# Ordering weight conversions and pooling around the row maxima of an attention and two feed-forward layers

## Chip, core and metric

One Trainium2 chip, one of its cores. The metric is device time in microseconds (us) of one execution; shorter is better.

## The reference

Pooled attention over 4 batches of 8 heads (1152 rows, head size 64), then two feed-forward layers on the 2304 pooled rows, all in float32:

```python
q_pool = q.reshape(B, H, S // 2, 2, D).mean(axis=3)
scores = np.matmul(q_pool, k.transpose(0, 1, 3, 2)) / sqrt(D)
scores -= scores.max(axis=-1, keepdims=True)
attn = np.exp(scores)
x = np.matmul(attn / (attn.sum(axis=-1, keepdims=True) + 1e-09), v)
x = x.transpose(0, 2, 1, 3).reshape(2304, 512)
h = x @ w_in;  x = (h - tanh(h)) @ w_out               # 512 -> 2048 -> 512
r = np.maximum(x @ w2_in, 0);  out = (s * r * r + b) @ w2_out
```

The kernel keeps float32 accuracy with matmuls of a narrower type by splitting operands into a high and a low part. The feed-forward weights arrive as raw words of two 32-bit halves each and are converted on the chip before they are split.

## The kernel before

The attention stage works on 16 pairs of heads (`n`; four pairs make a batch, `j` is the head in the pair). A head has nine score steps `t`: four matmuls on TensorE (PE) and two exponentials on ScalarE (ACT), into `pf`; every three steps a batch of matmuls multiplies `pf` with the values (`pv`). For the later heads GpSimd (POOL) adds the `pf` into two accumulators (L408), whose columns TensorE then sums; for the first four pairs and the last head TensorE sums them directly.

Around this a clock of ticks runs, four to a score step, so 72 to a pair where nothing stops it. At each tick `tick()` runs the work that has come due in `queue` (put there by `later(k, fn)`, k ticks ahead) and moves on the preparations of later pairs.

A preparation `prep(n)` is begun in pair n - 2, head 1, score step `NKT - LEAD // 4`. It pools the queries (two additions into `qr`, L265, on GpSimd from pair 1 on, and from pair 2 on behind the newest GpSimd addition traced, `added`), pauses four ticks, transposes queries (`ptq`, L271) and keys (`ptk`, L287) on TensorE, takes their low parts on VectorE (DVE; `ql`, `kl`), issues transfers that arrange the operands, and 16 ticks later loads the next pair. After a gap it computes the row maxima: 27 groups of one or two matmuls into a PSUM tile (`ptm`, L316) that VectorE reduces (`mp`, L317). The tag `pp` has three PSUM tiles, shared by maxima, transposes and the sweeps below.

`Weights.step` converts one unit of weights in six VectorE instructions (L195 to L207) from a raw tile (`raw`) that a transfer has filled, the last of them a copy into the weights; GpSimd subtracts for the low part (L210). Two ticks later the next load is traced. `CONVERT` and `CONVERT_AT` place 24 units on score steps of the first 13 pairs, four in each of the first four; 12 more follow in the last pair. A raw tile exists for each load under way: two in attention.

When a head's sum is there, `end` copies it on ScalarE, takes two reciprocals on VectorE (L453), eight ticks later multiplies (L458), splits into `xo` (ScalarE, then GpSimd, L460), and six ticks later stores it to DRAM (L464). From the second pair of the next batch on, a sweep (`sweep1`) loads a batch's results and does part of the first feed-forward layer between the attention's matmuls. After attention come the rest of that layer and then the second, both nearly pure TensorE work.

The framework orders each engine's instructions by priority, which follows the order of the trace, and by when its own model has them ready; an instruction that is ready sooner may be queued ahead of one traced before it. `tc.issue_after(ins)` queues what is traced inside it behind `ins` on the same engine, in order of issue only.

Of the kernel before, what the change touches and what calls it, by code (L numbers as in the profile page):

```python
# [10 lines left out]
F32R = mybir.dt.float32r  # L11
I32 = mybir.dt.int32
AF = mybir.ActivationFunctionType
ALU = mybir.AluOpType
AX = mybir.AxisListType
# [3 lines left out]
P = 128  # L19
# [10 lines left out]
LAST_STEPS = 4  # L30


LEAD = 20
GAP = 30
GAP1 = 12
MAXSTEP = 2
# [2 lines left out]
SUM = 2  # L39
GROUPS = ((0, 1, 2, 3, 4), (5, 6, 7, 8))  # L40
BATCH = 3
STORE, PUT = 8, 6

MOE_NS = 445
EVAC_NS = 250
AHEAD = 400
PFB = 10
SOON = 40
HOLD_NS = 8000
# [2 lines left out]
def f32(ap):  # L52
    return ap.bitcast(F32)
# [3 lines left out]
def attention_moe_moe_kernel(  # L57
# [19 lines left out]
    HB = SQ // 2  # L77
# [19 lines left out]
    act = nc.scalar.activation  # L97
    dve = nc.vector
    pool = nc.gpsimd
# [7 lines left out]
    fp = sctx.enter_context(tc.tile_pool(name="fin", bufs=1, side="right"))  # L107
# [10 lines left out]
    for i in range(4):  # L118
        g = i % 2
# [10 lines left out]

    clock = [0]
    moved = [None]
    added = [None]
    queue = []
    ticking = [True]

    def later(k, fn):
        queue.append((clock[0] + k, fn))
# [10 lines left out]
    def weight(which, f):  # L149
        return slots[w2slot[f] if which else f]  # L150

    class Weights:
# [32 lines left out]
        def step(self):  # L185
            if not self.loaded:
                return
            which, f, i, j, raw = self.loaded.popleft()
            w = weight(which, f)
            cols = slice(j * self.N, (j + 1) * self.N)  # L190
            lo, hi = raw[:, :, 0], raw[:, :, 1]
            t = self.pool.tile([P, self.N], I32, tag="t", name=f"t{which}_{f}_{i}_{j}", bufs=self.bufs)
            x = t.bitcast(F32)

            dve.tensor_scalar(out=t, in0=hi, scalar1=3, scalar2=0x3FFFFFFF,  # L195
                              op0=ALU.logical_shift_left, op1=ALU.bitwise_and)
            dve.scalar_tensor_tensor(out=t, in0=hi, scalar=-0x40000000, in1=t,  # L197
                                     op0=ALU.bitwise_and, op1=ALU.bitwise_or)
            dve.scalar_tensor_tensor(out=t, in0=lo, scalar=29, in1=t,  # L199
                                     op0=ALU.logical_shift_right, op1=ALU.bitwise_or)  # L200

            dve.tensor_scalar(out=hi, in0=hi, scalar1=1, scalar2=-0x80000000,
                              op0=ALU.logical_shift_left, op1=ALU.bitwise_xor)
            dve.scalar_tensor_tensor(out=x, in0=hi, scalar=float(-0x0FE00000), in1=x,
                                     op0=ALU.is_ge, op1=ALU.mult)
            if self.left > self.act_last:
                dve.tensor_copy(w[:, 2 * i, cols], x)  # L207
            else:
                act(w[:, 2 * i, cols], x, AF.Copy)  # L209
            added[0] = pool.tensor_sub(w[:, 2 * i + 1, cols], x, f32(w[:, 2 * i, cols]))  # L210
            later(RELOAD, self.load) if ticking else self.load()
            self.left -= 1
# [43 lines left out]
    def prep(n):  # L256

        T1, Uz, ql = T1s[n % 3], U1s[n % 3], qls[n % 2]
        U1 = [Uz[j][:, QOFF[j]:QOFF[j] + SQ] for j in range(2)]
        ops[n] = (T1, U1)  # L260

        for j in range(2):
            eng = dve if n == 0 else pool
            with tc.issue_after(added[0].ins) if n > 1 else ExitStack():
                eng.tensor_add(qrs[0][:, :, j * D:(j + 1) * D], qrs[j][:, :, 0:D], qrs[j][:, :, D:2 * D])  # L265
        yield 4
        for g in range(2):
            with tc.high_priority(offset=SOON):
                pt = psP.tile([P, KB], F32, tag="pp", name=f"ptq{n}_{g}")
                for i in range(3):  # L270
                    nc.tensor.transpose(  # L271
                        pt[:, i * QP:(i + 1) * QP],
                        qrs[0][:, 3 * g + i],
                        ident[:QP, :QP],
                    )
                act(U1[1][:, g * HB:(g + 1) * HB], pt[:, :HB], AF.Copy)
                dve.tensor_sub(
                    ql[:, g * HB:(g + 1) * HB], pt[:, :HB], f32(U1[1][:, g * HB:(g + 1) * HB])
                )
            yield 2  # L280
        for i in range(2):
            dma(out=f32(U1[0][i * D:(i + 1) * D, :]), in_=f32(U1[1][0:D, :]))
        for g in range(NKB):
            with tc.high_priority(offset=SOON):
                pt = psP.tile([P, KB], F32, tag="pp", name=f"ptk{n}_{g}")
                for i in range(3):
                    nc.tensor.transpose(  # L287
                        pt[:, i * P:(i + 1) * P],
                        kr[:, 3 * g + i].rearrange("p h d -> p (h d)"), ident)
                act(T1[1][:, g * KB:(g + 1) * KB], pt, AF.Copy)  # L290
                dve.tensor_sub(
                    kl[:, g * KB:(g + 1) * KB], pt, f32(T1[1][:, g * KB:(g + 1) * KB])
                )
            yield 2
        dma(out=f32(T1[0][0:D, :]), in_=f32(T1[1][0:D, :]))
        moved[0] = dma(out=f32(T1[0][D:P, :]), in_=f32(kl[0:D, :]))
        with tc.issue_after(moved[0].ins):
            dma(out=f32(U1[1][0:D, :]), in_=f32(U1[1][D:P, :]))
            dma(out=f32(T1[1][0:D, :]), in_=f32(kl[D:P, :]))
        if n + 1 < len(pairs):  # L300
            later(LOAD, lambda: load_pair(n + 1))
        yield GAP1 if n == 1 else GAP
        for j in range(2):
            ns = NQS + 1 - j
            mp = ap.tile([P, ns, NKB], F32, tag=f"mp{j}", name=f"mp{n}_{j}")
            m = ap.tile([P, ns], F32, tag=f"m{j}", name=f"m{n}_{j}")
            for s in range(ns):
                for i in range(NKB):
                    pt = psP.tile([P, KB], F32, tag="pp", name=f"ptm{n}_{j}_{s}_{i}")
                    kk = slice(i * KB, (i + 1) * KB)  # L310
                    if s == NQS:
                        mm(pt, Uz[0][:, s * P:(s + 1) * P], T1[0][:, kk], start=True, stop=False)
                        mm(pt, Uz[1][:, 0:P], T1[1][:, kk], start=False, stop=True)
                    else:
                        q0 = (s + j) * P
                        mm(pt, Uz[j][:, q0:q0 + P], T1[j][:, kk], start=True, stop=True)  # L316
                    dve.reduce_max(mp[:, s, i:i + 1], pt, axis=AX.X)  # L317
                    yield MAXSTEP
            dve.reduce_max(m, mp, axis=AX.X)
            pt = psP.tile([P, KB], F32, tag="pp", name=f"ptc{n}_{j}")  # L320
            nc.tensor.transpose(pt[:ns, :P], m, ident)
            act(cs[j], pt[:ns, :P], AF.Copy, scale=-1.0)
            maxes.add((n, j))
            yield 1
# [85 lines left out]
    def batch():  # L410
# [6 lines left out]
        po = pvt[n, j]  # L417
        with tc.high_priority(offset=AHEAD), tc.issue_after(last[0].ins):
            for i, (_, _, u, pf) in enumerate(reversed(todo)):
# [19 lines left out]
    xvs = {}  # L439
# [6 lines left out]
    def end(n, j, su):  # L446

        b, hp = pairs[n]
        ri = fp.tile([P, HB], F32, tag="ri", name=f"ri{n}_{j}", bufs=2)
        act(ri, su, AF.Copy, bias=1e-9)  # L450
        for g in range(2):
            x = slice(g * HB // 2, (g + 1) * HB // 2)
            dve.reciprocal(ri[:, x], ri[:, x])  # L453

        def store():
            xv = xvs.pop((n, j))
            xo = fp.tile([P, 2, HB], F32R, tag="xo", name=f"xo{n}_{j}", bufs=2)
            dve.tensor_mul(xv, xv, ri)  # L458
            act(xo[:, 0], xv, AF.Copy)
            pool.tensor_sub(xo[:, 1], xv, f32(xo[:, 0]))  # L460

            def put():
                for g in range(2):
                    dma(out=f32(x1d[b][hp][j * D:(j + 1) * D, :, g * HB:(g + 1) * HB]),  # L464
                        in_=f32(xo[g * D:(g + 1) * D]))
                placed.append((n, j))

            later(PUT, put)

        later(STORE, store)  # L470


# [38 lines left out]
    def gate1(pl_, ps, n, nm, bufs):  # L511
# [10 lines left out]

    load_pair(0)
    w1gen = Weights(stage, [[(0, f) for f in range(a, b)] for a, b in ((0, F1), (F1, FW), (FW, FA))],
                    2, 2, 2, LAST_STEPS)
    moe = deque()
    preps = deque()
    pend = deque()
# [43 lines left out]
    for n in range(len(pairs)):  # L572
# [3 lines left out]
        for j in range(2):  # L576
            for t in range(NKT):
                if j == 1 and t == NKT - LEAD // 4 and n + 2 < len(pairs):
                    add_prep(n + 2)
# [165 lines left out]
    for i in range(NBLK):  # L745
# [3 lines left out]
        for f in range(NFC):  # L749
            while w2gen.left > 2 * (NFC - 1 - f):  # L750
# [5 lines left out]
                                     op0=ALU.mult, op1=ALU.mult)  # L756
# [4 lines left out]
                                     op0=ALU.add, op1=ALU.subtract)  # L761
# [35 lines left out]
```

## Time and profile before

| | us |
|---|---|
| median of 3 runs (lowest to highest) | 1428.48 (1426.93 to 1430.91) |
| the profiled execution: its time | 1429.16 |
| its span, first to last instruction | 1427.4 |
| TensorE busy | 1359.7 (95%) |
| VectorE busy | 865.0 (61%) |
| ScalarE busy | 559.6 (39%) |
| GpSimd busy | 385.5 (27%) |

A busy time is that in which the engine runs at least one instruction. Where the engine that is busy nearly all the time waits, the time of the whole is lost; where another waits, nothing need be.

### The profile page before, as it was taken

Reading aid. Unit: us, or ns where it says so; the run is one execution under the profiler, and the core shown is the slowest. Engines: PE = TensorE matmul, PEld = TensorE weight load, DVE = VectorE, ACT = ScalarE, POOL = GpSimd, SP = SyncE. Lnnn points to the kernel's source line nnn. Section 1 sums busy time; section 2 is a strip of 40 time slices with the busy share of each in tenths; the row PEclk is TensorE's granted clock in tenths of the full one; section 3 lists DMA queues with packets and bytes.
Section 4 is the critical chain, followed back from the end, with each engine's and each line's share of the span. In section 5 each row is a group of like instructions: output and inputs, shape, how many; then the busy total and the mean of one; then the engine's idle time right before and its main releaser. Section 6 shows DMA issues by size and latency. Waiting matters only on the chain.

```text
span 1427.4 us, 23107 instructions
## 1 busy us (share of the span) xinstructions
PE 1359.7 (95%) x8670; PEld 1157.2 (81%) x8670; DVE 865.0 (61%) x1640; ACT 559.6 (39%) x1360; POOL 385.5 (27%) x311
## 2 busy tenths in 40 slices
PE   5999898999999999998989998999999999999998
PEld 3666666777777777776989997999899989898997
DVE  7877785667566664759796399844963232323232
ACT  2544445555455544544332233333332222323232
POOL 1212136565556645654220033100210000000000
PEclk9999999999999999999999999999999999999999
DMA  8756655563546555344776134744602020201000
GB/s 196 172 145 160 163 135 139 127 170 92 149 111 164 128 145 143 88 109 139 236 237 220 34 132 158 230 133 147 206 30 67 0 67 0 67 23 44 1 23 23
DMA packets 157647, 169.62 MB, mean 119 GB/s; under 512 B 52064, under 2 KB 130016, under 8 KB 157536
## 3 DMA queue, kind: packets, MB, share of 16 engines
q1 hardware_dynamic: 157536, 168.15, 42.8%
q8 instruction: 68, 1.11, 0.3%
q14 instruction: 43, 0.35, 0.1%
HBM read 101.98 MB, written 30.67 MB: 93 GB/s over the span
## 4 chain that ended last, share of the span: by engine, by line
PE 72%; DVE 16%; DMA 5%; POOL 3%; issue 3%; ACT 1%; SPq 1%; DVEq 0%; POOLq 0%; ACTq 0%
PE h L662 19%; PE o L735 14%; PE pv L421 9%; PE ptm L316 5%; PE y L673 5%; PE s L352 4%; PE s L353 4%; PE y L500 3%; PE h L487 2%; DVE t L199 2%; DMA raw<-in_moe_w_out_dram 2%; DVE t L197 2%; DVE mp L317 2%; DVE t L195 2%; POOL acc L408 2%
## 5 line engine op out<-in xcount | busy, mean ns | idle before, releaser
L662 PE MATMUL h<-xx,w 128*128 128x288 f32 (+1 forms) x2328 | 388.1, 316 | 1.7 <-DVE thb L514 1.7
L662 PEld LDWEIGHTS h<-xx,w 128*128 128x128 f32 x2328 | 365.1, 189 | 11.0 <-DVE thb L514 2.6
L317 DVE TENSOR_REDUCE mp<-ptm 128x1 f32<-128x384 f32 x432 | 225.2, 549 | 128.7 <-PE ptm L316 118.9
L354 ACT ACTIVATE pf<-s 128x288 f32<-128x288 f32 x576 | 220.8, 410 | 125.1 <-PE s L353 117.6
L210 POOL TENSOR_TENSOR w<-t,w 128x512 fp32r<-128x512 f32 (+1 forms) x82 | 98.0, 1195 | 381.4 <-ACT w L209 281.5
L673 PE MATMUL y<-ghb,w 128*128 128x288 f32 x784 | 174.5, 297 | 11.8 <-DVE yr L681 7.8
L408 POOL TENSOR_TENSOR acc<-acc,pf 128x576 f32<-128x576 f32 x115 | 166.3, 1446 | 64.8 <-ACT pf L354 60.0
L735 PE MATMUL o<-w,g2h 128*128 128x512 f32 x576 | 180.6, 395 | 0.0
L352 PE MATMUL s<-U,T 128*128 128x288 f32 x576 | 177.2, 314 | 0.6
L353 PE MATMUL s<-U,T 65*128 65x288 f32 x576 | 173.4, 309 | 1.1 <-DMA U<-c 1.1
L421 PE MATMUL pv<-pf,vo 128*64 128x288 f32 x1152 | 165.0, 423 | 0.0
L316 PE MATMUL ptm<-T,U 128*128 128x384 f32 x384 | 141.6, 387 | 16.6 <-DVE mp L317 10.8
L755 DVE SCALAR_TENSOR_TENSOR r<-r,sb 128x384 f32<-128x384 f32 x96 | 60.1, 626 | 140.7 <-ACT r L754 140.7
L673 PEld LDWEIGHTS y<-ghb,w 128*128 128x128 f32 x784 | 132.7, 190 | 13.5 <-DVE yr L681 8.9
L760 DVE SCALAR_TENSOR_TENSOR g2l<-r,sb,g2h 128x384 fp32r<-128x384 f32 x96 | 59.5, 620 | 111.1 <-ACT g2h L759 111.0
L421 PEld LDWEIGHTS pv<-pf,vo 128*64 128x64 f32 x1152 | 75.6, 139 | 59.6 <-ACT pf L354 10.6
L352 PEld LDWEIGHTS s<-U,T 128*128 128x128 f32 x576 | 111.6, 194 | 14.4 <-ACT pf L354 6.8
L735 PEld LDWEIGHTS o<-w,g2h 128*128 128x128 f32 x576 | 107.3, 188 | 18.0
L673 PE MATMUL y<-glb,w 128*128 128x288 f32 x392 | 117.0, 298 | 4.8 <-DVE glb L518 4.7
L353 PEld LDWEIGHTS s<-U,T 65*128 65x128 f32 x576 | 111.6, 194 | 5.9 <-issue 4.5
L735 PE MATMUL o<-w,g2l 128*128 128x512 f32 x288 | 114.1, 396 | 0.0
L759 ACT ACTIVATE g2h<-r,sb 128x384 fp32r<-128x384 f32 x96 | 59.5, 620 | 125.4 <-PE o L735 110.1
(78 smaller groups left out, 1747.6 us busy)
## 6 DMA issues: line engine op xcount, KB each, us to landing
xx<-x1d SPq DMA_DIRECT2D x80, 288.0 KB, 4.9
T<-T SPq DMA_DIRECT2D x48, 288.0 KB, 4.7
raw<-in_moe_w_in_dram SPq DMA_DIRECT2D x23, 512.0 KB, 3.7
raw<-in_moe_w_out_dram SPq DMA_DIRECT2D x23, 512.0 KB, 4.2
qr<-in_q_dram SPq DMA_DIRECT2D x32, 288.0 KB, 3.2
kr<-in_k_dram SPq DMA_DIRECT2D x32, 288.0 KB, 4.4
T<-kl SPq DMA_DIRECT2D x32, 288.0 KB, 4.2
vo<-in_v_dram SPq DMA_DIRECT2D x32, 288.0 KB, 5.0
```

Of the source, the lines that this page charges most:

```text
L210: added[0] = pool.tensor_sub(w[:, 2 * i + 1, cols], x, f32(w[:, 2 * i, cols]))
L316: mm(pt, Uz[j][:, q0:q0 + P], T1[j][:, kk], start=True, stop=True)
L317: dve.reduce_max(mp[:, s, i:i + 1], pt, axis=AX.X)
L352: last[0] = mm(ps, T1[j][:, t * P:(t + 1) * P], U1[j][:, sl], start=True, stop=False)
L353: last[0] = mm(ps, T2[j][:, t * P:(t + 1) * P], U2[j][:, sl], start=False, stop=True)
L354: act(pf[:, sl], ps, AF.Exp, scale=SCALE)
L408: added[0] = pool.tensor_add(accs[n, j, r], old, pf)
L421: mm(po[g * D:(g + 1) * D], vos[j][:, u], pf[:, g * HB:(g + 1) * HB], start=(t == 0 and i == 0), stop=(u == NKT - BATCH))
L662: mm(ps[:, :n], w[:, a, c * P:(c + 1) * P], xx[:, c, x, 0:n], start=(i == 0 and c == 0), stop=(i == 2 and c == NDC - 1))
L673: mm(ys[i][c], w[:, a, c * P:(c + 1) * P], x, start=(f == fa and r == 0), stop=(f == fb - 1 and r == 2))
L735: mm(ys[i][r], x[:, r * P:(r + 1) * P], w[:, a], start=(f == 0 and n == 0), stop=(f == NFC - 1 and n == 2))
L755: dve.scalar_tensor_tensor(out=r, in0=r, scalar=sb2[:, 0:1], in1=r, op0=ALU.mult, op1=ALU.mult)
```

## The change

The first of a conversion's instructions, the reciprocals and the product are each queued on VectorE behind the newest row maximum traced (`maxed`), and the low half of a result on GpSimd behind the newest addition (`added`). The reciprocals come two ticks later than before and the low half six ticks after the product, the store six ticks after that. The ties hold only while the clock of ticks runs. In attention four weight loads are under way instead of two. A preparation begins 12 ticks earlier, and from pair 2 on it pauses 16 ticks instead of four between pooling and transposes.

```diff
@@ -30,7 +30,7 @@
 LAST_STEPS = 4
 
 
-LEAD = 20
+LEAD = 32
 GAP = 30
 GAP1 = 12
 MAXSTEP = 2
@@ -39,11 +39,12 @@
 SUM = 2
 GROUPS = ((0, 1, 2, 3, 4), (5, 6, 7, 8))
 BATCH = 3
-STORE, PUT = 8, 6
+STORE, LOW, PUT = 8, 6, 6
 
 MOE_NS = 445
 EVAC_NS = 250
 AHEAD = 400
+RAWS = 4
 PFB = 10
 SOON = 40
 HOLD_NS = 8000
@@ -130,9 +131,14 @@
 
     clock = [0]
     moved = [None]
+    maxed = [None]
     added = [None]
     queue = []
     ticking = [True]
+
+    def behind(what):
+
+        return tc.issue_after(what[0].ins) if what[0] and ticking else ExitStack()
 
     def later(k, fn):
         queue.append((clock[0] + k, fn))
@@ -192,8 +198,9 @@
             t = self.pool.tile([P, self.N], I32, tag="t", name=f"t{which}_{f}_{i}_{j}", bufs=self.bufs)
             x = t.bitcast(F32)
 
-            dve.tensor_scalar(out=t, in0=hi, scalar1=3, scalar2=0x3FFFFFFF,
-                              op0=ALU.logical_shift_left, op1=ALU.bitwise_and)
+            with behind(maxed):
+                dve.tensor_scalar(out=t, in0=hi, scalar1=3, scalar2=0x3FFFFFFF,
+                                  op0=ALU.logical_shift_left, op1=ALU.bitwise_and)
             dve.scalar_tensor_tensor(out=t, in0=hi, scalar=-0x40000000, in1=t,
                                      op0=ALU.bitwise_and, op1=ALU.bitwise_or)
             dve.scalar_tensor_tensor(out=t, in0=lo, scalar=29, in1=t,
@@ -263,7 +270,7 @@
             eng = dve if n == 0 else pool
             with tc.issue_after(added[0].ins) if n > 1 else ExitStack():
                 eng.tensor_add(qrs[0][:, :, j * D:(j + 1) * D], qrs[j][:, :, 0:D], qrs[j][:, :, D:2 * D])
-        yield 4
+        yield 4 if n < 2 else 16
         for g in range(2):
             with tc.high_priority(offset=SOON):
                 pt = psP.tile([P, KB], F32, tag="pp", name=f"ptq{n}_{g}")
@@ -314,7 +321,7 @@
                     else:
                         q0 = (s + j) * P
                         mm(pt, Uz[j][:, q0:q0 + P], T1[j][:, kk], start=True, stop=True)
-                    dve.reduce_max(mp[:, s, i:i + 1], pt, axis=AX.X)
+                    maxed[0] = dve.reduce_max(mp[:, s, i:i + 1], pt, axis=AX.X)
                     yield MAXSTEP
             dve.reduce_max(m, mp, axis=AX.X)
             pt = psP.tile([P, KB], F32, tag="pp", name=f"ptc{n}_{j}")
@@ -448,16 +455,25 @@
         b, hp = pairs[n]
         ri = fp.tile([P, HB], F32, tag="ri", name=f"ri{n}_{j}", bufs=2)
         act(ri, su, AF.Copy, bias=1e-9)
-        for g in range(2):
-            x = slice(g * HB // 2, (g + 1) * HB // 2)
-            dve.reciprocal(ri[:, x], ri[:, x])
+
+        def invert():
+            with behind(maxed):
+                for g in range(2):
+                    x = slice(g * HB // 2, (g + 1) * HB // 2)
+                    dve.reciprocal(ri[:, x], ri[:, x])
+
+        xo = fp.tile([P, 2, HB], F32R, tag="xo", name=f"xo{n}_{j}", bufs=2)
 
         def store():
+            with behind(maxed):
+                dve.tensor_mul(xvs[n, j], xvs[n, j], ri)
+            act(xo[:, 0], xvs[n, j], AF.Copy)
+            later(LOW, low)
+
+        def low():
             xv = xvs.pop((n, j))
-            xo = fp.tile([P, 2, HB], F32R, tag="xo", name=f"xo{n}_{j}", bufs=2)
-            dve.tensor_mul(xv, xv, ri)
-            act(xo[:, 0], xv, AF.Copy)
-            pool.tensor_sub(xo[:, 1], xv, f32(xo[:, 0]))
+            with behind(added):
+                pool.tensor_sub(xo[:, 1], xv, f32(xo[:, 0]))
 
             def put():
                 for g in range(2):
@@ -467,6 +483,7 @@
 
             later(PUT, put)
 
+        later(2, invert)
         later(STORE, store)
 
 
@@ -522,7 +539,7 @@
 
     load_pair(0)
     w1gen = Weights(stage, [[(0, f) for f in range(a, b)] for a, b in ((0, F1), (F1, FW), (FW, FA))],
-                    2, 2, 2, LAST_STEPS)
+                    2, RAWS, 2, LAST_STEPS)
     moe = deque()
     preps = deque()
     pend = deque()
```

## Rows read from the trace of the kernel before

**Rows 1.** By stretch, busy us of PE, PEld, DVE, ACT, POOL; clock, DMA, GB/s.

```profile
60.00:120.00 60.00, 55.69 (x397) 36.91 (x395) 48.53 (x110) 28.49 (x77) 13.55 (x16) 0.97 0.64 157
900.00:1427.00 527.00, 518.03 (x2895) 477.87 (x2893) 219.20 (x388) 158.60 (x313) 21.86 (x15) 1.00 0.21 69
```

**Rows 2.** TensorE's waits, 190 to 655 us: total, times, longest.

```profile
PE ptq L271 <- POOL qr L265: 9.0, 3, 3.5
```

**Rows 3.** GpSimd, 203 to 224 us: start, duration, instruction, [idle before <-releaser].

```profile
214.96 1.42 POOL L408 TENSOR_TENSOR acc<-pf,pf 128x576 f32<-128x576 f32 x1 [8.19 <-ACT pf L354]
216.45 2.99 POOL L408 TENSOR_TENSOR acc<-acc,pf 128x576 f32<-128x576 f32 x2
219.40 2.05 POOL L265 TENSOR_TENSOR qr<-qr 96x384 f32<-96x384 f32 x2
```

**Rows 4.** Stretches behind the three waits for pooling, each with an equal one after it.

```profile
221.50:227.00 5.50, 5.49 (x24) 4.87 (x26) 2.34 (x5) 3.14 (x8) 2.17 (x3) 0.50 0.54 148
227.00:232.50 5.50, 5.50 (x38) 4.13 (x36) 3.84 (x9) 3.21 (x8) 2.94 (x3) 1.00 0.45 109
380.60:384.10 3.50, 3.50 (x18) 3.48 (x17) 1.26 (x3) 1.69 (x5) 1.82 (x2) 0.51 0.60 169
384.10:387.60 3.50, 3.50 (x27) 2.41 (x26) 1.39 (x4) 1.25 (x4) 1.40 (x1) 1.00 0.66 161
542.00:547.90 5.90, 5.88 (x26) 5.11 (x28) 1.99 (x4) 2.35 (x6) 2.59 (x3) 0.50 0.52 136
547.90:553.80 5.90, 5.90 (x43) 4.67 (x41) 3.16 (x7) 3.63 (x10) 2.50 (x3) 1.00 0.27 75
```

**Rows 5.** TensorE's waits, 60 to 190 us.

```profile
PE ptm L316 <- DVE mp L317: 9.3, 5, 2.9
```

**Rows 6.** TensorE in order of time, the matmuls behind three of these waits.

```profile
92.13 0.44 PE L316 MATMUL ptm<-T,U 128*128 128x384 f32 x1 [2.91 <-DVE mp L317]
...
131.52 0.69 PE L316 MATMUL ptm<-T,U 128*128 128x384 f32 x1 [2.36 <-DVE mp L317]
...
174.23 0.44 PE L316 MATMUL ptm<-T,U 128*128 128x384 f32 x1 [1.55 <-DVE mp L317]
```

**Rows 7.** VectorE's waits, 60 to 190 us.

```profile
DVE t L195 <- DMA raw<-in_moe_w_out_dram: 8.3, 4, 4.1
DVE t L195 <- DMA raw<-in_moe_w_in_dram: 5.1, 1, 5.1
```

**Rows 8.** VectorE in order of time, 82 to 95 and 163 to 176 us.

```profile
87.99 0.29 DVE L195 TENSOR_SCALAR t<-raw 128x256 int32<-128x256 int32 x1 [3.27 <-DMA raw<-in_moe_w_out_dram]
...
89.90 0.29 DVE L207 CAST w<-t 128x256 fp32r<-128x256 f32 x1
...
162.73 3.92 DVE L317 TENSOR_REDUCE mp<-ptm 128x1 f32<-128x384 f32 x8 [0.84 <-PE ptm L316]
171.75 0.29 DVE L195 TENSOR_SCALAR t<-raw 128x256 int32<-128x256 int32 x1 [5.10 <-DMA raw<-in_moe_w_in_dram]
...
174.09 1.96 DVE L453 RECIPROCAL ri<-ri 128x144 f32<-128x144 f32 x2
```

**Rows 9.** All engines, 20 to 60 us.

```profile
20.00:60.00 40.00, 38.77 (x258) 26.65 (x258) 34.62 (x81) 16.80 (x46) 5.86 (x7) 0.96 0.80 183
```

**Rows 10.** VectorE in order of time, 4 to 20 us.

```profile
8.60 0.29 DVE L195 TENSOR_SCALAR t<-raw 128x256 int32<-128x256 int32 x1 [2.59 <-DMA raw<-in_moe_w_in_dram]
...
9.39 0.42 DVE L199 SCALAR_TENSOR_TENSOR t<-raw,t 128x256 int32<-128x256 int32 x1
...
10.80 0.81 DVE L277 TENSOR_TENSOR ql<-ptq,U 128x288 fp32r<-128x288 f32 x2
...
13.88 1.18 DVE L199 SCALAR_TENSOR_TENSOR t<-raw,t 128x256 int32<-128x256 int32 x1
```

**Rows 11.** TensorE's waits, 0 to 60 us.

```profile
PE ptk L287 <- DVE ql L277: 2.1, 1, 2.1
```

**Rows 12.** GpSimd in order of time, 4 to 20 us.

```profile
13.79 0.98 POOL L265 TENSOR_TENSOR qr<-qr 96x384 f32<-96x384 f32 x1
```

## The prediction

> **What bounds the kernel now.** I read the busy time by stretches first. From 900 us to the end TensorE is busy 518.03 of 527 us at the full clock, so nothing that this change touches can shorten that stage. The attention stage is different: between 60 and 120 us TensorE is busy 55.69 of 60 us and VectorE 48.53 of 60 [rows 1]. TensorE is the bound in both, but in attention it also stands still now and then, and its waits say for whom. So the change is worth what it takes out of those waits, and what the clock loses behind them; everything after attention merely starts earlier.
>
> Next I read TensorE's waits from 190 to 655 us. The largest group is the transposes of the pooled queries: 9.0 us in three waits for GpSimd's pooling [rows 2]. GpSimd's order of time shows why: it stands idle for 8.19 us until 214.96, then makes three accumulations, and only then the two pooling additions, 219.40 to 221.45 [rows 3]. TensorE's transposes start right behind them. The pooling had been placed behind additions that were themselves waiting for ScalarE's exponentials.
>
> The waits have a second price. Right after each of the three, the granted clock is 0.50 or 0.51, the lower of the two levels (1.2 GHz), and TensorE gets through fewer matmuls than in the stretch of equal length behind it: 24 against 38, 18 against 27, 26 against 43 [rows 4].
>
> In the first pairs of heads the other thing shows. From 60 to 190 us TensorE waits 9.3 us in five waits for row maxima [rows 5]; three of them are 2.91, 2.36 and 1.55 us long [rows 6]. In the same stretch VectorE waits 8.3 + 5.1 us for raw weights at the first step of a conversion [rows 7]. Its order of time puts the two together: it stands idle 3.27 us before 87.99 and 5.10 us before 171.75, then converts, and behind the conversion come one maximum and a pair of reciprocals (1.96 us) before the maxima go on [rows 8]. Conversions that wait for a load block the maxima queued behind them, and TensorE runs out of PSUM tiles.
>
> **Part 1, pooling 12 ticks earlier (lead 20 to 32, pause 4 to 16).** The transposes stay at the same tick, so do the loads of the next pair; only the two additions move. At the new tick the newest addition traced is the last of the head before, which ended before the idle stretch began (214.96 - 8.19 = 206.77 us). So 2.05 us of pooling fits into 8.19 us of idle time and ends some 10 us before TensorE needs it; the three accumulations then come when they came before. Gain: 9.0 us of waits. The clock: at the full rate the 24, 18 and 26 matmuls would have taken 24/38 x 5.5 = 3.5, 18/27 x 3.5 = 2.3 and 26/43 x 5.9 = 3.6 us, so 2.0 + 1.2 + 2.3 = 5.5 us were lost. I count both: **14.5 us**. Bounds: nothing if the pooling stays behind the same accumulations, 14.5 if it leaves no wait.
>
> **Part 2, four raw loads and conversions tied behind the newest maximum.** With four loads under way the load has two more units' time to land, so the 8.3 + 5.1 us that VectorE stands idle should go, and with them the three waits of 2.9 + 2.4 + 1.5 = 6.8 us. Of the other two of the five (9.3 - 6.8 = 2.5 us), which I can't tie to a load, I count half. Together **8.0 us**, between 0 and 9.3. The lower clock behind these waits I don't count. The two further loads at the start use the DMA engines, which are busy 0.80 of 20 to 60 us [rows 9], so they find room; if they didn't, the operands' transfers in that stretch would be late.
>
> The tie takes something away too. Now VectorE makes conversions before the first maxima: from 8.60 us on, while the first query correction waits until 10.80 [rows 10], and TensorE waits 2.1 us for it [rows 11]. Tied behind a maximum, these units go later. Between 0 and 2.1 us come free; I take **1.0**, since transfers follow. One unit takes 2.2 us (87.99 to 90.19) [rows 8]; three make 6.6 us, and between 20 and 60 us VectorE has 40 - 34.62 = 5.4 us idle [rows 9]. So 1.2 us doesn't fit and will come out as waits for maxima, and conversions that bunch up behind one maximum may cost another wait or so: I keep back **3.0 us**, between 0 and 6.
>
> **Part 3, reciprocals, products and low halves.** The reciprocals come two ticks later, the low half six ticks later and behind the newest addition. One tick is about (380.6 - 221.5) / 288 = 0.55 us, since these two waits are four pairs of 72 ticks apart [rows 4]. The reciprocals' two ticks lie inside the eight that the product waits anyway, so a result is stored six ticks, 3.3 us, later, and by what the ties add. The sweep that reads it starts only with the second pair of the next batch, a pair (40 us) after the last head, and that cover is far longer. I count nothing. If it were gone, the sweep would wait up to 3.3 us in each of three batches. What is queued behind the tied reciprocal on VectorE are later maxima only, and these gain: a pair of 1.96 us no longer gets in ahead of them.
>
> A rule of the Trainium skill speaks against moving work on GpSimd. A conversion step that takes 0.42 us at 9.39 took 1.18 us at 13.88 [rows 10], and GpSimd's pooling addition of 0.98 us ran from 13.79 [rows 12]. "SBUF — State Buffer" (section "SBUF: two separate sides") says the port pair that VectorE and GpSimd share is an exclusive lock: a VectorE instruction with two SBUF inputs waits for the whole GpSimd instruction. The row agrees with it, and by that rule each moved addition could hold a conversion. It is rival E.
>
> **The sum.** 14.5 + 8.0 + 1.0 - 3.0 = 20.5 us. Against the profiled execution's 1429.16 us (span 1427.4): **1408.7 us**. The median of the runs, 1428.48, lies 0.7 us below that execution, which is inside the spread of the runs.
>
> **The rivals.** A: the conversions' stalls only move. VectorE is at 48.5 of 60 us in these pairs, which speaks for it; its idle time before loads speaks against. Then 14.5 + 1.0 - 3.0 = 12.5 us remain: 1416.7.
> B: everything goes, at the upper ends, and the clock also stays up behind the three conversion waits (1.8 us each, the mean of the three measured): 14.5 + 9.3 + 2.1 + 5.5 = 31.4, 1397.8. Against it: some wait usually comes up in another place.
> C, slower: tied conversions bunch into the maxima's phases. Maxima follow each other at 3.92 / 8 = 0.49 us [rows 8]; if two of them are all the slack that three PSUM tiles give, a unit of 2.2 costs TensorE 1.2 us, and 24 units 29.3 us, against 14.5 + 9.3 taken out: 5.5 us more, 1434.7. It decides from 23.8 / 24 = 1.0 us a unit on. For it speaks how full VectorE is from 20 to 60 us; against it, that the units already run among maxima there and TensorE waits little.
> D: the change doesn't do what it says: the pooling still lands behind the same accumulations and the ties repeat the order that is there. A couple of us at most: 1427.
> E: earlier poolings meet conversions in four pairs (2 to 5), two additions each, at 1.18 - 0.42 = 0.76 us: 6.1 us less gain, 1414.8. Against it: the poolings meet conversions today as well.
>
> **How the numbers follow.** Forecast 0.42, A 0.20, E 0.12, B 0.10, C 0.08, D 0.08. The forecast's own range, from its bounds, is 1402 to 1416. The 8-in-10 range goes from a little below B to where D begins, 1395 to 1426; C and most of D lie outside. A change of 0.3% (4.3 us) is about what the runs can tell from none. Faster by more than that are the forecast, A, B and E nearly whole: 0.82. Within it: D and the edges of C and the forecast: 0.10. Slower: 0.08.
>
> **What would show it.** Right: the pooling stands at the start of GpSimd's idle stretch, TensorE has no wait of over 1 us for it, and the granted clock stays 1.00 near 220, 380 and 540 us; VectorE's wait for raw weights between 60 and 190 us falls under 3 us, TensorE's for maxima there to 2 or 3 us. Wrong: new waits for maxima between 20 and 60 us of more than 3 us, a wait of the sweeps for their input, or poolings that still end just before the transposes.

## The result, and the profile after

The changed kernel takes 1445.61 us (median of 4 runs, 1439.32 to 1445.99) against 1427.70 for the kernel before (4 runs, 1426.26 to 1430.91): a ratio of 1.0112, 95% interval 1.0079 to 1.0145. By the ratio it is slower by 16 us, where 20.5 us less had been forecast. Its profiled execution took 1445.91 us, with a span of 1444.1.

Waits first. In the rows of the changed kernel the maximum is L324 (L317 before), its matmul L323, a conversion's first step L202. These are TensorE's waits of the changed kernel from 0 to 60, from 60 to 190 and from 190 to 655 us, then VectorE's from 60 to 190 us, all its rows (columns: total, times, longest):

```profile
PE ptm L323 <- DMA T<-kl: 6.6, 1, 6.6
...
PE ptk L294 <- DVE ql L284: 0.4, 1, 0.4
...
PE ptm L323 <- DVE mp L324: 8.3, 10, 1.8
...
PE ptc L328 <- DVE m L326: 6.9, 4, 1.9
PE ptm L323 <- DVE mp L324: 4.6, 7, 1.3
...
DVE mp L324 <- PE ptm L323: 47.8, 18, 6.1
```

Two of the named signs came true. The wait of the query transposes for pooling [rows 2] has no row any more between 190 and 655 us, and VectorE's wait for raw weights [rows 7] is gone. The wait of the first key transposes for the query correction fell as well, from 2.1 [rows 11] to 0.4 us. But TensorE's waits for maxima have not gone: 8.3 us in ten pieces from 60 to 190 us, where there were 9.3 in five [rows 5], and behind 190 us 6.9 + 4.6 us, where the kernel before had 2.7 + 1.5:

```profile
PE ptc L321 <- DVE m L319: 2.7, 4, 1.0
PE ptm L316 <- DVE mp L317: 1.5, 3, 0.6
```

The sign that was named for a wrong forecast, new waits for maxima of over 3 us between 20 and 60 us, did not come; the loss lies elsewhere. VectorE itself now waits 47.8 us for TensorE's products (11.1 + 2.8 us in the kernel before, 20.0 in the kernel without the tie, below): each of the two engines waits for the other.

The stretches show the clock and the rate. All engines of the changed kernel (window, length, busy time and instructions of PE, PEld, DVE, ACT, POOL; then clock, DMA share, GB/s): 20 to 60 and 60 to 190 us, the first head of the third pair (2.0), three short stretches inside it, and the places of the three poolings of [rows 4].

```profile
20.00:60.00 40.00, 38.21 (x225) 26.29 (x228) 30.58 (x74) 16.49 (x43) 5.69 (x7) 0.87 0.73 165
60.00:190.00 130.00, 120.76 (x790) 77.33 (x791) 82.11 (x192) 55.85 (x153) 20.25 (x24) 0.92 0.53 137
...
110.68:135.61 24.93, 21.29 (x134) 13.18 (x138) 17.15 (x44) 9.01 (x24) 5.91 (x7) 0.89 0.65 167
...
126.60:130.30 3.70, 0.89 (x2) 0.37 (x2) 3.70 (x10) 0.00 (x0) 2.49 (x3) 1.00 0.74 219
130.30:137.10 6.80, 6.43 (x28) 2.92 (x28) 2.60 (x7) 1.13 (x3) 2.67 (x3) 0.50 0.60 157
137.10:143.90 6.80, 6.80 (x44) 5.17 (x41) 4.88 (x9) 3.59 (x10) 0.00 (x0) 1.00 0.42 126
...
215.70:225.90 10.20, 8.24 (x21) 5.01 (x23) 8.98 (x18) 0.71 (x2) 3.86 (x5) 0.50 0.62 158
375.00:395.00 20.00, 19.99 (x139) 15.79 (x139) 13.28 (x24) 10.14 (x28) 12.72 (x10) 1.00 0.57 151
535.00:560.00 25.00, 24.46 (x165) 19.55 (x164) 17.40 (x31) 12.21 (x33) 14.47 (x13) 1.00 0.70 178
```

From 20 to 60 us the clock is 0.87 where it was 0.96 [rows 9], with VectorE less busy than before, 30.58 against 34.62 us. In the short stretches TensorE is busy for 0.89 of 3.70 us while VectorE is busy throughout; then 6.8 us at 0.50, the lower level, with 28 matmuls, where the next 6.8 us hold 44. It is the picture of [rows 4], now behind waits for maxima instead of pooling. Where the poolings had cost the clock, it is 1.00 near 380 and 540 us, but still 0.50 near 220; in front of that stand waits of TensorE for maxima, 1.50 us before 213.29 and 1.17 before 215.69.

What VectorE does in that place, in order of time (start, duration, instruction, [idle before <-releaser]), and under it TensorE, each of the changed kernel:

```profile
122.18 0.29 DVE L202 TENSOR_SCALAR t<-raw 128x256 int32<-128x256 int32 x1
123.71 0.56 DVE L324 TENSOR_REDUCE mp<-ptm 128x1 f32<-128x384 f32 x1 [1.24 <-PE ptm L323]
124.19 0.41 DVE L204 SCALAR_TENSOR_TENSOR t<-raw,t 128x256 int32<-128x256 int32 x1
124.52 0.29 DVE L202 TENSOR_SCALAR t<-raw 128x256 int32<-128x256 int32 x1
...
126.67 0.55 DVE L324 TENSOR_REDUCE mp<-ptm 128x1 f32<-128x384 f32 x1
127.13 0.50 DVE L211 SCALAR_TENSOR_TENSOR t<-raw,t 128x256 f32<-128x256 int32 x1
127.56 0.88 DVE L202 TENSOR_SCALAR t<-raw 128x256 int32<-128x256 int32 x1
```

```profile
127.28 0.44 PE L323 MATMUL ptm<-T,U 128*128 128x384 f32 x1 [0.98 <-DVE mp L324]
129.50 0.45 PE L323 MATMUL ptm<-T,U 128*128 128x384 f32 x1 [1.78 <-DVE mp L324]
130.56 1.49 PE L323 MATMUL ptm<-T,U 128*128 128x384 f32 x2 [0.62 <-DVE mp L324]
```

One unit's first step runs at 122.18. Then VectorE idles 1.24 us for a product, and only after the maximum of 123.71 come that unit's next step, 124.19, and the first step of the next unit, 124.52. From 124.19 to 126.67 the steps of two units run, and only then the next maximum; three times TensorE waits for one, 0.98, 1.78 and 0.62 us. VectorE idles first and converts when the maxima are due. (The step at 127.56 is a tied one as well; it comes behind the maximum of 126.67.)

### The profile page after: what moved, and what is told of

The parts are those of the page before. It is cut to its first block, busy times and chain, and to the rows that moved or that the text cites. A ratio compares the mean times of both kernels' runs of the same rounds, so it can differ in the third digit from the quotient of the medians.

```text
span 1444.1 us, 23130 instructions
## 1 busy us (share of the span) xinstructions
PE 1371.7 (95%) x8670; PEld 1159.3 (80%) x8670; DVE 863.8 (60%) x1640; ACT 560.1 (39%) x1360; POOL 385.2 (27%) x311
## 4 chain that ended last, share of the span: by engine, by line
PE 73%; DVE 19%; DMA 4%; issue 2%; ACT 1%; SPq 0%; POOL 0%; DVEq 0%; ACTq 0%
PE h L679 19%; PE o L752 14%; PE pv L428 9%; PE ptm L323 5%; PE y L690 5%; PE s L360 4%; PE s L359 4%; PE y L517 3%; DVE t L206 3%; DVE t L204 2%; PE h L504 2%; DVE mp L324 2%; DVE t L202 2%; PE su L394 2%; DVE t L211 2%
## 5 line engine op out<-in xcount | busy, mean ns | idle before, releaser
L324 DVE TENSOR_REDUCE mp<-ptm 128x1 f32<-128x384 f32 x432 | 228.9, 550 | 181.4 <-PE ptm L323 174.5
L428 PE MATMUL pv<-pf,vo 128*64 128x288 f32 x1152 | 169.3, 431 | 0.0
L323 PE MATMUL ptm<-T,U 128*128 128x384 f32 x384 | 147.3, 400 | 20.1 <-DVE mp L324 12.9
L323 PEld LDWEIGHTS ptm<-T,U 128*128 128x128 f32 x384 | 73.8, 196 | 46.4 <-DVE mp L324 22.5
```

The source lines that it names most:

```text
L324: maxed[0] = dve.reduce_max(mp[:, s, i:i + 1], pt, axis=AX.X)
L428: mm(po[g * D:(g + 1) * D], vos[j][:, u], pf[:, g * HB:(g + 1) * HB], start=(t == 0 and i == 0), stop=(u == NKT - BATCH))
```

## The experiments

Each comparison ran on one chip beside the kernel before, whose medians in the four groups were 1428.98, 1429.16, 1427.11 and 1430.08 us; ratios are to these, with their 95% intervals. Sizes are differences of medians. T1 puts the loss on the tie of the conversions; the theories against it are named in the expectations.

### The tie taken away, and alone

`no_conv_tie`: the changed kernel with the first step of a conversion free.

```diff
-            with behind(maxed):
-                dve.tensor_scalar(out=t, in0=hi, ...
+            dve.tensor_scalar(out=t, in0=hi, ...
```

> The changed kernel without the tie of the conversions; the ties of reciprocals, products and low halves stay, and four loads. T1 expects the first thirteen pairs to lose their new waits, some 24 us: about 1421, the last pair still slow. T2 expects no change or little: 1440 to 1446. T3 the same as T2.

1400.02 us, ratio 0.9795 (0.9759 to 0.9832). The tie costs 45.6 us in this kernel, nearly twice what T1 had expected.

`conv_tie_only`: the kernel before, with `maxed` and this tie and nothing else of the change.

> The kernel before with the conversions' tie alone (two loads, old pooling). T1 expects the whole loss of the first thirteen pairs, 24 us: about 1450. T2 expects no loss beyond a few us: 1428 to 1432. T3: 1428.

1444.36 us, ratio 1.0112 (1.0079 to 1.0144): 15.4 us slower. The tie alone makes a kernel slower too, by a third of the 45.6. VectorE's waits from 60 to 190 us, all its rows, bear on why it is only a third:

```profile
DVE mp L323 <- PE ptm L322: 48.0, 21, 5.3
```

The waits for raw weights that the kernel before has there [rows 7] are gone under the tie, with two loads and the stores at their old place. So the tie mends something too, and that cannot be gained a second time by loads or stores.

`two_raws`: the changed kernel with two loads.

```diff
-RAWS = 4
+RAWS = 2
```

> The changed kernel with two weight loads under way instead of four. Theory T1 (the tie of the conversions puts them among the row maxima) expects only the last pair to mend, some 9 us: about 1436. Theory T2 (four loaded units make VectorE convert in bunches) expects the first pairs to mend too: about 1412. T3 (tied reciprocals and products) expects 1445 or 1436.

1433.24 us, ratio 1.0029 (1.0007 to 1.0050). Two loads take back 12.4 us under the tie, not the whole. So in the changed kernel the third and fourth load cost 12.4 us, where the prediction had them gain. In the profiled executions some 6 us of it lie in the last head, which takes 30.8 us with four loads and 24.4 with two, from its first exponential to its last `pv` matmul.

`no_ties`: the changed kernel with no tie at all.

```diff
-        return tc.issue_after(what[0].ins) if what[0] and ticking else ExitStack()
+        return ExitStack()
```

> The changed kernel without any of the new ties (conversions, reciprocals, products, low halves), with four loads, the earlier pooling and the later ticks of reciprocals and low halves. If four loads and the pooling make the gain of the kernel without the conversions' tie, and the other ties do nothing: 1400 us. If these ties keep reciprocals out of the way of maxima, some pairs get their waits back: 1405 to 1412.

1402.05 us, ratio 0.9807 (0.9790 to 0.9824). Beside 1400.02 the other ties, on the reciprocals, products and low halves, are worth some 2 us, and the intervals overlap.

### What about the tie costs

Here the conversions by head, in three kernels: the changed one, `no_conv_tie`, and `tie_older` (below). The rows are the instructions that write or read `t` (five of a unit's six on VectorE, and GpSimd's subtraction); the heads are 1.1, 2.0 and 2.1 (pair and head); columns: window, length, busy (x count) of VectorE, ScalarE and GpSimd, clock, DMA share, GB/s. First the changed kernel:

```profile
90.98:110.68 19.70, 0.00 (x0) 0.00 (x0) 0.00 (x0) 0.95 0.35 92
110.68:135.61 24.93, 7.18 (x20) 0.00 (x0) 3.03 (x4) 0.89 0.65 167
135.61:155.20 19.59, 0.00 (x0) 0.00 (x0) 0.00 (x0) 0.96 0.36 92
```

`no_conv_tie`:

```profile
86.54:105.52 18.98, 5.00 (x14) 0.00 (x0) 1.58 (x2) 1.00 0.68 192
105.52:123.03 17.51, 5.76 (x17) 0.00 (x0) 2.44 (x3) 1.00 0.79 186
123.03:142.22 19.19, 6.40 (x19) 0.00 (x0) 3.17 (x4) 1.00 0.64 182
```

`tie_older`:

```profile
83.42:102.41 18.99, 4.99 (x14) 0.00 (x0) 1.60 (x2) 1.00 0.64 162
102.41:120.14 17.73, 2.00 (x6) 0.00 (x0) 1.48 (x2) 1.00 0.76 185
120.14:139.34 19.20, 4.97 (x14) 0.00 (x0) 1.59 (x2) 1.00 0.57 139
```

Tied, all four units of a pair (4 x 5 = 20) run in its first head, and none in the second; that head takes 24.9 us, of which TensorE is busy 21.29 (above). Free, they run in both heads, 14 to 19 instructions in each of these, and VectorE takes up units of later pairs as their weights are there: the same head takes 17.5 us. The two heads 1.1 and 2.0 together take 44.63 us with 20 of these instructions against 36.49 us with 31: 8.1 us more with fewer conversions in them.

`tie_spread`: the changed kernel with the places of the four units spread over both heads.

```diff
-CONVERT_AT = (0, 2, 4, 6, 8, 10, 12, 14, 16)
+CONVERT_AT = (0, 9, 4, 13, 6, 11, 2, 15, 17)
```

> The changed kernel, ties and all, with the four conversions of a pair at score steps 0, 9, 4 and 13, so two for each head instead of four for the first. In the trace of the changed kernel all tied units run in the first head of a pair (4, 0, 4, 0), untied ones in both. T1a (they bunch in one head) expects most of the loss in the first four pairs to go: 1425 to 1432. T1b (a unit queued right behind a maximum delays the next maxima wherever it stands) expects 1440 to 1447.

1427.24 us, ratio 0.9994 (0.9972 to 1.0016): 18.4 us of the 45.6 come back. Bunching in one head is less than half of it, if all that the spreading mends is put down to it.

`tie_older`: the changed kernel, the tie kept but behind an older maximum, the sixteenth newest (so the units before the sixteenth maximum are free).

```diff
+    older = deque([None] * 16, 16)
...
-            with behind(maxed):
+            with behind(older):
...
+                    older.append(maxed[0])
```

> The changed kernel with conversions tied behind the maximum that was traced 16 before the newest. The units may then move ahead of up to 16 maxima into earlier idle time. If what the tie takes away is this moving ahead: most of the loss goes, 1402 to 1418. If any tie to maxima hurts: 1440.

1405.38 us, ratio 0.9848 (0.9825 to 0.9871): 40.2 us come back. In its rows above the units are unevenly spread too, 14 and 6, but most of them run one head earlier, and its heads take 17.7 to 19.2 us. So a tie as such costs little, and an uneven spread need not cost. What costs is that a unit cannot start before the *newest* maximum and so comes when the next maxima are due.

`tie_late`: only units from the seventeenth on are tied.

```diff
-            with behind(maxed):
+            with behind(maxed if self.left <= 20 else [None]):
```

> The changed kernel with the conversions' tie only from the 17th unit on (pair 4 and later), the first 16 free. T1 (each tied unit costs by its place among the maxima) expects the loss in proportion to the heads that still have tied units (pairs 4, 5, 9 to 12: some 20 of 45 us): 1418 to 1422. If the loss comes from the start, where the conversions are moved out of the first microseconds: 1400 to 1405.

1423.73 us, ratio 0.9963 (0.9940 to 0.9985): 23.7 us over `no_conv_tie`, half the cost, with the start and the first pairs free. The start alone is not the place of the cost.

### The gains: pooling, loads, results

`pool_only`: the kernel before with the earlier pooling alone.

```diff
-LEAD = 20
+LEAD = 32
...
-        yield 4
+        yield 4 if n < 2 else 16
```

> The kernel before with the earlier pooling alone (lead 32, pause 16). All theories agree that the three waits for pooling and the slow clock behind them go: 1412 to 1415 us, about 14 below the kernel before. If the earlier pooling is itself what costs time in the first pairs, no gain, 1428 or more.

1414.90 us, ratio 0.9907 (0.9876 to 0.9938): 14.1 us, where 14.5 was forecast.

`pool_raws`: that, with four loads instead of two.

> The kernel before with the earlier pooling and four loads, nothing else. If four loads take out the waits for raw weights in the first pairs, as I had forecast: 1400 to 1404, like the kernel without ties. If the later ticks of reciprocals and low halves did it: 1412 to 1416, like the pooling alone.

1411.59 us, ratio 0.9898 (0.9864 to 0.9932). Four loads are worth 3.3 us here by the medians and 1.3 by the ratios, and the intervals overlap; 8.0 had been the term.

`free_two_raws`: `no_conv_tie` with two loads.

> No tie of the conversions, ties of the results kept, two loads instead of four. If the four loads take out VectorE's waits for raw weights (13.4 us in the first pairs) and with them TensorE's waits for maxima, they come back here: 1412 to 1415, as with the earlier pooling alone. If the tied reciprocals did it: 1395 to 1400, since the last pair is also better with two loads.

1396.31 us, ratio 0.9767 (0.9748 to 0.9785). The expectation fell: without four loads it is no slower than `no_conv_tie`, rather 3.7 us faster, though the intervals overlap. It has the lowest median of all, 32.9 us under the kernel before and 49.3 under the changed one.

`free_last_two`: `no_conv_tie`, four loads, but only two in the last pair.

```diff
-            later(RELOAD, self.load) if ticking else self.load()
+            if self.ahead < 4 or self.left not in (14, 13):
+                later(RELOAD, self.load) if ticking else self.load()
```

> No tie of the conversions, four loads, but two in the last pair, where conversions come at every score step. If units that are ready too soon block the sweep's gates and the additions there (TensorE's waits of 2.8 and 2.7 us and the low clock behind them), the last pair falls back from 27.9 to about 21.5 us for its second head: 1393 to 1395. If not: 1400.

1399.13 us, ratio 0.9793 (0.9776 to 0.9810): no gain, a miss.

`ticks_two_raws`: pooling and the later ticks of the results; no ties, two loads.

> Earlier pooling, later ticks of reciprocals and low halves, two loads, no ties at all. If the ties of reciprocals and products are what mended the first pairs with two loads: 1412 to 1416. If the later ticks alone did it: 1396 to 1399.

1398.51 us, ratio 0.9807 (0.9786 to 0.9827): 16.4 us less than `pool_only`, from ticks that the prediction counted at nothing. Two runs take them apart.

`recip_late`: `ticks_two_raws` with the low half back at its place; the reciprocals alone are two ticks later.

```diff
-            later(LOW, low)
+            low()
```

> Earlier pooling, two loads, no ties, reciprocals two ticks later, low half and store at their old ticks. If the reciprocals are what got in ahead of the maxima: 1396 to 1401, and VectorE's waits for raw weights gone. If the stores held up the queue of transfers: 1411 to 1416.

1413.01 us, ratio 0.9893 (0.9865 to 0.9920): nothing clear of noise beyond pooling.

`low_late`: the other half; low half and store six ticks later.

```diff
-        later(2, invert)
+        invert()
```

> Earlier pooling, two loads, no ties, low half and store six ticks later, reciprocals at their old tick. If the transfer queue stood before stores whose data was not there, and raw loads behind them came late: 1396 to 1401. If the reciprocals did it: 1411 to 1416.

1400.40 us, ratio 0.9794 (0.9753 to 0.9836): 12.6 us less than `recip_late`, beside the same kernel before, and 14.5 less than `pool_only`. So the gain lies in the later low half and store. SyncE's queue of transfers in order of time, first of `pool_only`, then of `low_late` (start, duration, transfer):

```profile
84.15 0.58 SPq L181 DMA_DIRECT2D raw<-in_moe_w_out_dram  x1
...
90.66 0.33 SPq L181 DMA_DIRECT2D raw<-in_moe_w_out_dram  x1
101.28 1.21 SPq L464 DMA_DIRECT2D x1d<-xo  x2
102.58 2.09 SPq L181 DMA_DIRECT2D raw<-in_moe_w_out_dram  x2
```

```profile
83.96 0.43 SPq L187 DMA_DIRECT2D raw<-in_moe_w_out_dram  x1
...
92.48 1.20 SPq L480 DMA_DIRECT2D x1d<-xo  x2
94.79 1.07 SPq L187 DMA_DIRECT2D raw<-in_moe_w_out_dram  x2
```

In `pool_only` the queue stands from 91.0 to 101.28 before the store of a result that GpSimd has not made yet, and two loads of raw weights come out only behind it, at 102.58. In `low_late`, which is 2.5 us ahead by then, the queue stands before the store from 86.0 to 92.48, and the two loads behind it go out at 94.79, 7.8 us sooner. VectorE's and TensorE's waits from 60 to 190 us, first of `pool_only`, then of `low_late`, are the other end:

```profile
DVE t L195 <- DMA raw<-in_moe_w_out_dram: 8.2, 3, 4.1
DVE t L195 <- DMA raw<-in_moe_w_in_dram: 5.1, 1, 5.1
...
PE ptm L316 <- DVE mp L317: 10.5, 7, 3.0
```

```profile
DVE mp L324 <- PE ptm L323: 18.9, 16, 3.6
...
PE ptm L323 <- DVE mp L324: 2.9, 2, 1.5
```

The 8.2 + 5.1 us of waits for raw weights have no row in `low_late`, with two loads under way, and TensorE's 10.5 us of waits for maxima are 2.9. But the load that VectorE waited for in `pool_only` is not one of those behind the late store. It is an earlier one, of 84.15, and in `low_late` it goes out at 83.96: no sooner, and with the 2.5 us counted even later in its head. What changed is the order of VectorE's own queue, again first `pool_only`, then `low_late`:

```profile
88.75 0.29 DVE L195 TENSOR_SCALAR t<-raw 128x256 int32<-128x256 int32 x1 [3.69 <-DMA raw<-in_moe_w_out_dram]
...
91.97 0.55 DVE L317 TENSOR_REDUCE mp<-ptm 128x1 f32<-128x384 f32 x1
```

```profile
86.15 0.56 DVE L324 TENSOR_REDUCE mp<-ptm 128x1 f32<-128x384 f32 x1 [3.62 <-PE ptm L323]
...
91.79 0.81 DVE L202 TENSOR_SCALAR t<-raw 128x256 int32<-128x256 int32 x1
```

In `pool_only` the conversion stands ahead of the maxima, and VectorE waits 3.69 us for its load. In `low_late` seven maxima, the reciprocals and the product stand ahead of it, and it starts 7.8 us after its load went out. The same holds a pair and two pairs later: in `pool_only` the conversions of 133.19 and 176.09 wait 4.09 and 5.06 us for loads of 128.90 and 171.22; in `low_late` those of 128.50 and 165.25 come behind maxima, 7.8 and 6.2 us after their loads. So the stall goes because the maxima no longer stand behind a conversion that waits, not because loads come sooner. Why a later store changes this order is not shown; the framework queues by what its own model has ready, and no run here records that model.

## Why the prediction was wrong

**What bounds the kernel: right.** TensorE's waits in attention, with the clock behind them, decided here as well. Between the changed kernel and `no_conv_tie` the spans differ by 1444.1 - 1398.9 = 45.2 us. Their mean clocks are 0.976 and 0.992, so by estimate 1444.1 x 0.024 - 1398.9 x 0.008 = some 23 us of it are lower clock. The busy times agree: TensorE is busy 1371.7 against 1347.2 us with the same 8670 matmuls, 24.5 us longer, and it is idle 20.7 us longer (72.4 against 51.7).

**Part 1, pooling: right.** 14.1 us measured alone, 14.5 forecast, with the waits and the low clock behind them gone in `pool_only`.

**Part 2, the tie: the step that failed.** It is "conversions that bunch up behind one maximum may cost another wait or so: I keep back **3.0 us**, between 0 and 6". The tie cost 15.4 us alone, 36.9 with everything else but two loads (`two_raws` against `free_two_raws`) and 45.6 in the changed kernel. I had priced the units that run before the first maxima and asked whether 6.6 us fit into VectorE's idle time from 20 to 60 us. What I did not ask is where the other units run when nothing ties them. The framework may queue an instruction that is ready ahead of one traced before it, and in `no_conv_tie` it does so across heads, which fills the times in which VectorE waits for products. The tie forbids just that. The total idle time of VectorE was no measure of the room, since the tie decides which part of it may be used.

**Rival C had the mechanism and the sign,** at a chance of 0.08. Its price of 1.2 us a unit was low: 45.6 / 24 = 1.9 us, well over the 1.0 from which it decides. By the split above, an estimate, the waits are 0.9 us of that and the clock behind them 1.0, and C had priced waits alone. What spoke against it, that the units already run among maxima between 20 and 60 us, was read from units that nothing tied, and did not carry over to tied ones.

**Part 2, four loads: a second step that failed.** That "the load has two more units' time to land" was to bring 8.0 us. In the changed kernel the two further loads cost 12.4 us: under the tie there was no wait for raw weights left to mend (`conv_tie_only`), and the last head became longer. Without the tie they cut VectorE's waits for raw weights from 13.3 to 3.6 us (`pool_only`, `pool_raws`), and the last head begins 12.7 us sooner in these two executions; there the 8.0 was even low. Yet the medians differ by 3.3 us only, and on top of the later stores by -3.7. The later stores mend the same waits, so the gains do not add. And something is given back in the last head: it takes 27.7 us with four loads against 23.5 with two. TensorE's waits there, first with two loads, then with four:

```profile
PE su L434 <- POOL acc L408: 2.8, 1, 2.8
PE y L500 <- ACT gha L517: 1.1, 1, 1.1
```

```profile
PE su L434 <- POOL acc L408: 2.9, 1, 2.9
PE s L352 <- ACT pf L354: 1.6, 1, 1.6
PE su L387 <- ACT pf L354: 0.7, 1, 0.7
```

New with four loads are two waits for ScalarE's exponentials, 1.6 and 0.7 us (the wait of `y` lies behind attention, at 663.84). That ready conversions get ahead of what ScalarE needs is argued, not shown: `free_last_two`, which should have mended it, did not.

**Part 2, the start: given back at once.** The wait for `ql` fell by 1.7 us, but the first maxima then waited 6.6 us for the transfer of `kl` (first row of the first view above), where they had waited 5.4 us in the kernel before (put down there to a conversion). All of TensorE's waits from 0 to 60 us come to 15.6 us in both kernels. The 1.0 us did not come, as the sentence "since transfers follow" feared.

**Part 3: not nothing.** "I count nothing" followed only the reader of the results, the sweep, a pair of heads later. With the low half and the store six ticks later VectorE's queue has the maxima ahead of the conversions, and 1414.9 - 1400.4 = 14.5 us come free without the tie. So the reading "Conversions that wait for a load block the maxima queued behind them" was right, and the order was the cure, more than the loads. SyncE's queue does stand before late stores, 30.6 us for `xo` between 60 and 190 us in the kernel before and 19.1 in `low_late`; but that this is what made VectorE wait is not shown, since the loads in question went out no sooner. The reciprocals' two ticks are worth nothing clear of noise.

**The sum by what was measured:** 1429.0 - 14.1 (pooling) - 14.5 (later stores) + 45.6 (tie) = 1446.0 us, against 1445.6. Since the 45.6 is the changed kernel less `no_conv_tie`, this says no more than that `no_conv_tie` and `low_late` take the same time. With the tie first the shares are others: 1429.0 + 15.4 (tie) - 11.1 (pooling and results, `conv_tie_only` to `two_raws`) + 12.4 (four loads). The parts do not add, and each price holds beside what stood there when it was taken. The range that was stated "from its bounds" was also narrower than these: everything at its best, 14.5 + 9.3 + 2.1, gives 1403.3, and nothing gained with 6 lost gives 1435.2, not 1402 and 1416. The measured time lies beyond either.

**Rival E** was not tried by itself. One row bears on it: the step at 127.56 took 0.88 instead of 0.29 us. By the Trainium skill's "SBUF — State Buffer" (section "SBUF: two separate sides") a VectorE instruction in a mode that uses two ports and a GpSimd instruction lock a shared port pair against each other for the whole of the one that starts first. The trace agrees in so far as a GpSimd subtraction ran from 127.31 for 0.97 us; which mode the step was in no run shows. Pooling came out near its forecast, 14.1 for 14.5. But in the profiled executions `pool_only` is 3.4 us behind the kernel before at the first exponential of head 4.0 (214.5 against 211.1) and gains its time behind it, so a loss of a few us in the first pairs, from this or something else, is not ruled out.

**Open:** why the last head is longer with four loads, with the tie and without it; why later stores change the order on VectorE; and the cost of the start under the tie by itself, which no run separates.

## What to carry to other kernels

A tie "behind the newest" is a ban on filling idle time ahead of it: before pricing one, count per stage where the untied instructions run now and where they would, and tie, if at all, to something old enough to leave the gap usable. Where an engine waits for a load, ask what stands behind the waiting instruction in its own queue: with ready work placed ahead of it the wait was gone here, though the load came no sooner, and that was worth more than more buffers. Two cures for one wait are to be counted once, and a tie can be one of them.

## What the runs showed that was not expected

Three short waits of TensorE within four microseconds (0.98, 1.78 and 0.62 us) were followed by a granted clock of 0.50 for 6.8 us, as the waits for pooling had been [rows 4]; broken-up waits were followed by the lower level here too. And VectorE's waits for weights, which I had put down to loads that come too late, went when the loads came no sooner: six ticks more for a store on another queue changed the order of conversions and maxima on VectorE, and with it 14.5 us.
